# A table prefetch of five items and a rule for empty steps, in a Fourier, mixing and feed-forward kernel on one core

## The chip, the cores and the metric

The kernel runs on one core of a Trainium2 chip. The metric is the device time of one execution in microseconds (us), the median of three runs. The core's engines are called as the profile calls them: PE is TensorE (matrix products; PEld its weight loads), DVE is VectorE, ACT is ScalarE, POOL is GpSimd, SP is SyncE, which here does nothing but issue transfers. Each engine works through its own queue of instructions in order; the engines wait for each other by semaphores.

## The reference: what is computed

```python
X = np.fft.rfft(x, axis=1)                  # x: 8 batches x 3072 x 256
Yr = Xr @ w_r - Xi @ w_i + b_r
Yi = Xr @ w_i + Xi @ w_r + b_i
Yr = np.sign(Yr) * np.maximum(np.abs(Yr) - lam, 0.0)      # lam = 0.01; Yi alike
y = np.fft.irfft(Yr + 1j * Yi, n=3072, axis=1)
h = y.reshape(-1, 256) @ w_in               # 256 x 2048, float64 weights
g = h * np.tanh(softplus(h))
out = g @ w_out                             # 2048 x 256, float64 weights
```

Each of eight batches is transformed along its 3072 rows, mixed by two complex 256 x 256 products, cut softly at 0.01, transformed back, and sent through a feed-forward layer of width 2048.

## The kernel before, in words

**Precision.** Products run on pairs: a 32-bit value is split into `hi` (rounded to the engine's float32r format) and `lo` (the rest). `split` (L185) makes a pair: the copy that rounds (L187 on VectorE, L189 on ScalarE), then the subtraction that gives `lo` (L190, VectorE).

**The transform of a batch** is a `chain` of four segments, each a list of items:

- first (k = 0): 7 items `item_a`, products of x with a small table, result to DRAM scratch s1;
- second (k = 1): 12 items `item_b` (one block of frequencies each, with a table `tt` of 256 KB from DRAM, two tables for block 11, which comes first), each followed one place later by an `item_m` (mix, cut off, store y to scratch s3). The 24 items stand as b11, b0, m11, b1, m0, b2, m1 and so on;
- third (k = 2): 13 items `item_c` (first half of the way back; four or more loads each from s3, result to scratch s2);
- fourth (k = 3): `item_f` 0 and 1 (second half of the way back, with a table `vt`; result `yh`, `yl` in SBUF). There are 12 such items in a batch, two for each chunk of 512 rows.

An item has `load` (its transfers, on SP's queue), `cload` (its table, on POOL's queue), `prep` (the split) and `mm` (one or two groups of matmuls with what follows them). The tables `tt` and `vt` share a pool of four buffers (`p_t`), the loads after the first batch one of four (`p_ld`).

**`run_chain` (L696)** sets the order. It is a generator: each `yield` is one step. For every segment it issues the first loads and tables, then yields empty steps, then calls `prep` of the first one or two items, yields empty steps again (the line of the change), and then takes one `mm` group per step; ahead of each item `ahead` calls `load`, `cload` and `prep` of later items: `ahead_n` loads, `cla` tables, two preps ahead (one in the first segment).

**The first batch** (b = 0) runs alone, from L838 on, with `gap` 0 (no empty steps), `ahead_n` 6 and `cla` 3. The tables of the second segment's first three items are called early, when 11 steps are done. Between the steps, VectorE turns the float64 weights into pairs (`aux_steps`). In this batch half of each item's y stores go over POOL's queue, the queue that also carries the tables.

**The main loop (L867)** then runs over tiles t, 96 per batch (six chunks of 16 tiles). Tile t has `ffn1(t)`: six matmuls of L748 on one 128-column block of `w_in`, and the activation `s`; on even tiles the split of `s` for two tiles (L762, L763); one step of transform work; and `ffn2(t - 4)`: four pairs of matmuls of L778 and L779. The step of transform work comes from one of two generators:

- `gen`, the chain of the next batch, started at the batch's first tile with `gap` 2; its fourth segment is held back until tile 82 of the batch;
- `extra`, a chain of one segment with one item: in tiles 2 and 8 of each of the first five chunks, items `item_f` 2 to 11 of the running batch, also with `gap` 2. In a tile in which `extra` has a real step, `gen` has none; in its empty steps `gen` goes on.

```python
c = tt // KFF
if tt % KFF in (2, 8) and c < 5:
    extra = run_chain([[item_f(b, 2 * c + 2 + (tt % KFF) // 8)]], gap=2)
```

The schedule is written out by hand: the order of calls is the order of each engine's queue. All SP transfers of both generators and of the output stand in one queue.

Of the kernel before, what the change touches and what calls it, by code (L numbers as in the profile page):

```python
# [128 lines left out]
def fft_mix_ffn_kernel(ctx: ExitStack, tc: tile.TileContext, x, w_r, w_i, b_r, b_i, w_in, w_out,  # L129
# [71 lines left out]
    def setup_dft():  # L201
        nc.gpsimd.dma_start(out=fa, in_=c_fa)

    def setup_u():
        nc.gpsimd.dma_start(out=uu, in_=c_u)
# [3 lines left out]
    def load_mix():  # L209
        for k in range(2):  # L210
            t = p_y.tile([128, 2, 512], F32, tag=("yh", "yl")[k], name="wraw").rearrange("p a f -> p (a f)")[:, 0:512]
            nc.sync.dma_start(out=t[:, 0:256], in_=w_r[k * 128:(k + 1) * 128, :])
            nc.sync.dma_start(out=t[:, 256:512], in_=w_i[k * 128:(k + 1) * 128, :])
            mixraw.append(t.rearrange("p (s c) -> p s c", s=2))
# [5 lines left out]
    def setup_mix():  # L220
        for k in range(2):
            src = mixraw[k]
            hi, lo = wmix[:, k, 0, 1:3, :], wmix[:, k, 1, 1:3, :]
            split(src, hi, lo, "s")
            for s in range(2):
                nc.scalar.activation(out=wmix[:, k, s, 0, :], in_=f32(wmix[:, k, s, 2, :]), func=ACTF.Copy, scale=-1.0)
# [55 lines left out]
    def weight_jobs():  # L282
        def w1(k, n):
            sl = slice(n * 512, (n + 1) * 512)
            return (w_in.bitcast(I32)[k * 128:(k + 1) * 128, n * 1024:(n + 1) * 1024],
                    *(win[:, k, s, sl].rearrange("p (a c) -> p a c", a=2) for s in range(2)), False)

        def w2(n):
            return (w_out.bitcast(I32)[n * 256:(n + 1) * 256, :].rearrange("(k p) c -> p k c", p=128),
                    *(wout[:, 2 * n:2 * n + 2, s, :] for s in range(2)), True)  # L290

        order = [w1(0, 0), w1(1, 0), w1(0, 1), w1(1, 1), w2(0), w2(1), w1(0, 2), w1(1, 2), w2(2), w2(3),
                 w1(0, 3), w1(1, 3), w2(4), w2(5), w2(6), w2(7)]
        return [FromDouble(n, *a) for n, a in enumerate(order)]
# [15 lines left out]
    def tick():  # L310
        while pend:
            pend.pop(0)()
# [368 lines left out]
    def chain(b):  # L681
        segs = [[item_a(b, p) for p in range(7)]]
        bm = []
        order = [11] + list(range(11))
        bs = [item_b(b, k) for k in order]
        for k in range(12):
            bm.append(bs[k])
            if k:
                bm.append(item_m(b, order[k - 1], bs[k - 1]))
        bm.append(item_m(b, order[11], bs[11]))  # L690
        segs.append(bm)
        segs.append([item_c(b, p) for p in (*range(8), 12, *range(8, 12))])
        segs.append([item_f(b, 0), item_f(b, 1)])
        return segs

    def run_chain(segs, ahead_n=3, ahead_a=2, cla=2, gap=0, hold=None, on_seg=None):  # L696


        for k, seg in enumerate(segs):
            while hold is not None and k == len(segs) - 1 and hold():  # L700
                yield None
            n = len(seg)
            at = [0, 0, 0]
            la, pla = (ahead_a, 1) if k == 0 and n == 7 else (ahead_n, 2)

            def ahead(i):
                for s, (d, f) in enumerate(((la, "load"), (cla, "cload"), (pla, "prep"))):
                    while at[s] < min(n, i + d):
                        getattr(seg[at[s]], f)()
                        at[s] += 1  # L710

            while at[1] < min(n, cla):
                seg[at[1]].cload()
                at[1] += 1
            while at[0] < min(n, la):
                seg[at[0]].load()
                at[0] += 1
            if on_seg is not None:
                on_seg(k)
            last = k == len(segs) - 1  # L720
            for _ in range(gap + (4 if k == 2 else 1 if last else 0) if gap else 0):
                yield None
            while at[2] < min(n, pla):
                seg[at[2]].prep()
                at[2] += 1
            for _ in range((2 if last or k == 1 else 1) if gap else 0):
                yield None
            for i in range(n):
                ahead(i + 1)
                for f in seg[i].mm:  # L730
                    tick()
                    f()
                    yield k
            tick()
# [59 lines left out]
    with tc.manual_schedule():  # L794
        setup_dft()
        aux = weight_jobs()
        top = [2]
        n_raw = [0]

        def aux_load(m):  # L800
            while n_raw[0] < min(m, len(aux)):
                aux[n_raw[0]].load()
                n_raw[0] += 1

        def aux_run():
            for n, job in enumerate(aux):
                aux_load(n + 1)
                for k, _ in enumerate(job.work(aux[n - 1] if n else None)):
                    if k == 5:
                        aux_load(min(n + (4 if n + 3 <= N_EARLY else 3), top[0]))  # L810
                    yield
            yield from aux[-1].finish()

        aux_gen = aux_run()
        n_aux = [0]

        def aux_steps(m):
            for _ in range(m):
                if started[0] or n_aux[0] < 9 * N_EARLY - 2:
                    next(aux_gen, None)  # L820
                    n_aux[0] += 1

        def on_seg(k):
            if k == 1:
                top[0] = N_EARLY
                aux_load(4)
                setup_mix()
                aux_steps(6)
            elif k == 2:
                aux_steps(12)  # L830
            elif k == 3:
                aux_steps(10)

        PACE = (1.6, 0.9, 1.4, 2)
        first = chain(0)
        cnt = 0
        owed = 0.0
        for k in run_chain(first, ahead_n=6, ahead_a=3, cla=3, on_seg=on_seg):  # L838
            cnt += 1
            if cnt in (2, 6):  # L840
                aux_load(1 + (cnt > 2))
            if cnt == 8:
                load_mix()
                load_bias()
            if cnt == 11:
                for it in first[1][:3]:
                    it.cload()
            if cnt == 20:
                setup_u()
            if cnt == 57:  # L850
                for it in first[3]:
                    it.cload()
            if cnt > 4:
                owed += PACE[k]
            while owed >= 1:
                aux_steps(1)
                owed -= 1
        aux_steps(9 * len(aux))
        started[0] = True
        top[0] = len(aux)  # L860

        LAG = 4
        NT = NCH * KFF
        NS = 6 * KFF
        gen = None
        extra = None
        for t in range(NT + LAG):  # L867
            tt = t % NS
            b = t // NS
            if t == 0:  # L870
                aux_load(N_EARLY + 2)
            if t < 18:
                aux_steps(3)
            if t == 18:
                aux_steps(18)
                mix_gauss()
            if t < NT:
                if tt == 0:
                    gen = run_chain(chain(b + 1), gap=2, hold=lambda: hold[0]) if b + 1 < NB else None
                hold = [tt < 5 * KFF + 2]  # L880
                ffn1(t)
# [3 lines that stand above are left out]
            if t % 2 == 0 and t // 2 - 1 in s_t:  # L885
                split_g(t // 2 - 1, t < 18)
            did = None
            if extra is not None:
                did = next(extra, -1)
                if did == -1:  # L890
                    extra = did = None
            if did is None and gen is not None and t < NT:
                did = next(gen, -1)
                if did == -1:
                    gen = None
            if t < NT and tt == NS - 1 and gen is not None:
                hold = [False]
                for _ in gen:
                    pass
                gen = None  # L900
            if t >= LAG:
                ffn2(t - LAG)
# [26 lines left out]
```

## Time and profile before

| | us |
|---|---|
| median of three runs | 2815.71 (2812.26 to 2817.09) |
| profiled execution | 2812.9 |
| its span | 2811.1 |
| TensorE busy | 2739.7 (97%) |
| VectorE busy | 1952.8 (69%) |
| ScalarE busy | 951.2 (34%) |
| chain that ended last: share of TensorE | 87% |

The busy time of an engine is the time in which at least one of its instructions ran. TensorE's matmuls overlap in their pipeline, so one matmul's duration is longer than the distance to the next. In a list of waits, "A <- B" says that A stood idle until B had ended. In a timeline, an instruction's idle time before it stands in brackets with what ended it; "x2" says that two alike were merged.

### The profile page before, as it was taken

Reading aid. Unit: us, or ns where it says so; the run is one execution under the profiler, and the core shown is the slowest. Engines: PE = TensorE matmul, PEld = TensorE weight load, DVE = VectorE, ACT = ScalarE, POOL = GpSimd, SP = SyncE. Lnnn points to the kernel's source line nnn. Section 1 sums busy time; section 2 is a strip of 40 time slices with the busy share of each in tenths; the row PEclk is TensorE's granted clock in tenths of the full one; section 3 lists DMA queues with packets and bytes.
Section 4 is the critical chain, followed back from the end, with each engine's and each line's share of the span. In section 5 each row is a group of like instructions: output and inputs, shape, how many; then the busy total and the mean of one; then the engine's idle time right before and its main releaser. Section 6 shows DMA issues by size and latency. Waiting matters only on the chain.

```text
span 2811.1 us, 39281 instructions
## 1 busy us (share of the span) xinstructions
PE 2739.7 (97%) x14782; PEld 2333.5 (83%) x14782; DVE 1952.8 (69%) x3294; ACT 951.2 (34%) x1947; POOL 148.0 (5%) x274
## 2 busy tenths in 40 slices
PE   6779999999999999999999999999999999999999
PEld 5558888888888888888888888888888888888887
DVE  5788866778667776678766777567766778655553
ACT  4333333333333333333333333323333333333232
POOL 1400000000000000000000000000000000000000
PEclk9789999999999999999999999999999999999999
DMA  7643324333233323342233332433324333231000
GB/s 223 204 143 86 94 70 120 102 90 94 72 112 109 99 80 86 101 121 84 76 106 102 104 84 68 120 106 87 90 75 120 98 91 91 78 95 42 27 27 16
DMA packets 170388, 266.38 MB, mean 95 GB/s; under 512 B 22518, under 2 KB 67590, under 8 KB 170198
## 3 DMA queue, kind: packets, MB, share of 16 engines
q1 hardware_dynamic: 122806, 173.75, 20.6%
q0 software_dynamic: 33536, 64.95, 8.6%
q10 hardware_dynamic: 13856, 25.17, 3.1%
q8 instruction: 117, 1.92, 0.3%
q14 instruction: 73, 0.60, 0.1%
HBM read 163.10 MB, written 100.68 MB: 94 GB/s over the span
## 4 chain that ended last, share of the span: by engine, by line
PE 87%; DVE 5%; DMA 3%; SPq 2%; issue 1%; ACT 1%; POOL 0%; ACTq 0%; DVEq 0%; POOLq 0%
PE hp L748 35%; PE acc L778 23%; PE acc L779 12%; PE psp L518 4%; PE psa L345 2%; PE psc L626 2%; SPq L604 2%; PE psk L499 2%; PE psf L666 2%; PE psb L434 2%; DMA ld<-in_x_dram 1%; DMA ld<-s 1%; PE psf L667 1%; DVE lo L190 1%; PE psb L436 1%
## 5 line engine op out<-in xcount | busy, mean ns | idle before, releaser
L778 PE MATMUL acc<-wout,gh 128*128 128x512 f32 x3072 | 1115.7, 397 | 0.0
L748 PE MATMUL hp<-yh,win 128*128 128x512 f32 x3072 | 1082.1, 393 | 4.9 <-ACT yh L675 4.6
L753 ACT ACTIVATE s<-hp 128x512 f32<-128x512 f32 x768 | 458.5, 597 | 1368.7 <-PE hp L748 1283.3
L779 PE MATMUL acc<-wout,gl 128*128 128x256 f32 x3072 | 859.2, 280 | 0.0
L748 PEld LDWEIGHTS hp<-yh,win 128*128 128x128 f32 x3072 | 578.6, 188 | 137.4 <-ACT yh L675 4.8
L778 PEld LDWEIGHTS acc<-wout,gh 128*128 128x128 f32 x3072 | 576.6, 188 | 123.4 <-issue 6.0
L748 PE MATMUL hp<-yl,win 128*128 128x512 f32 x1536 | 604.1, 393 | 0.0
L779 PEld LDWEIGHTS acc<-wout,gl 128*128 128x128 f32 x3072 | 577.5, 188 | 16.3
L763 DVE TENSOR_TENSOR gl<-s,gh 128x1024 fp32r<-128x1024 f32 x384 | 470.5, 1225 | 65.3 <-PE acc L779 26.1
L762 DVE CAST gh<-s 128x1024 fp32r<-128x1024 f32 x376 | 258.7, 688 | 207.1 <-ACT s L753 207.1
L748 PEld LDWEIGHTS hp<-yl,win 128*128 128x128 f32 x1536 | 289.2, 188 | 35.0 <-DVE yl L676 0.4
L190 DVE TENSOR_TENSOR lo<-ld,hi 120x512 fp32r<-120x512 f32 (+3 forms) x390 | 269.7, 692 | 31.8 <-ACT hi L189 16.3
L187 DVE CAST hi<-ld 120x512 fp32r<-120x512 f32 (+2 forms) x367 | 154.7, 422 | 56.5 <-DMA ld<-s 55.5
L670 DVE TENSOR_TENSOR eo<-psf,cor 128x256 f32<-128x256 f32 x192 | 76.9, 422 | 117.5 <-ACT cor L669 116.8
L783 DVE TENSOR_TENSOR ot<-acc,oc 128x256 f32<-128x256 f32 x192 | 72.8, 420 | 98.2 <-ACT oc L782 98.2
L650 POOL DMA_DIRECT2D vt<-in_c_v_dram x96 | 52.5, 547 | 1609.4 <-PE psf L667 1261.1
L518 PE MATMUL psp<-wmix,xh 128*128 128x256 f32 x672 | 133.2, 281 | 0.0
L676 DVE TENSOR_TENSOR yl<-yt,yh 128x512 fp32r<-128x512 f32 x96 | 66.5, 693 | 67.1 <-ACT yh L675 67.1
L518 PEld LDWEIGHTS psp<-wmix,xh 128*128 128x128 f32 x672 | 109.1, 188 | 3.6
L675 ACT ACTIVATE yh<-yt 128x512 fp32r<-128x512 f32 x96 | 60.7, 632 | 145.4 <-DVE yt L673 145.4
L626 PE MATMUL psc<-hi,uu 120*120 120x512 f32 (+1 forms) x224 | 89.0, 412 | 17.2 <-ACT hi L189 14.8
L666 PE MATMUL psf<-vt,hi 128*128 128x256 f32 x384 | 95.4, 325 | 7.5 <-ACT hi L189 7.5
(114 smaller groups left out, 2630.5 us busy)
## 6 DMA issues: line engine op xcount, KB each, us to landing
ld<-s SPq DMA_DIRECT2D x185, 256.0 KB
tt<-in_c_t_dram POOLq DMA_DIRECT2D x104, 256.0 KB, 3.2
vt<-in_c_v_dram POOLq DMA_DIRECT2D x96, 256.0 KB, 3.0
out_dram<-ot SPq DMA_DIRECT2D x48, 512.0 KB
ld<-in_x_dram SPq DMA_DIRECT2D x90, 240.0 KB
s<-ev ACTq DMA_DIRECT2D x89, 240.0 KB
s<-y SPq DMA_DIRECT2D x330, 64.0 KB
ld<-s SPq DMA_DIRECT2D x350, 60.0 KB
```

Source lines behind the costliest of these rows:

```text
L187: nc.vector.tensor_copy(out=hi, in_=src)
L190: nc.vector.tensor_tensor(out=lo, in0=src, in1=f32(hi), op=ALU.subtract)
L518: nc.tensor.matmul(out=it.ps[:, ri * 256:(ri + 1) * 256], lhsT=m[:, c, 130 - ri * 128:258 - ri * 128], rhs=wmix[:, c, s, 2 * ri, :], start ...
L626: nc.tensor.matmul(out=ps[:K, sl], lhsT=uu[:K, var, s, :K], rhs=m[:K, sl], start=n == 0, stop=n == 2)
L666: nc.tensor.matmul(out=ps[:, p], lhsT=it.hi[:, q:q + 128], rhs=it.v[:, p], start=True, stop=False)
L670: nc.vector.tensor_tensor(out=eo[:, c], in0=ps[:, :, 0], in1=cor, op=ALU.add)
L748: nc.tensor.matmul(out=hp, lhsT=win[:, k, s, f * 128:(f + 1) * 128], rhs=m[:, k, :], start=n == 0, stop=n == 5)
L753: nc.scalar.activation(out=s_t[t // 2][:, t % 2, :], in_=hp, func=ACTF.Mish)
L762: nc.vector.tensor_copy(out=gh, in_=s)
L763: nc.vector.tensor_tensor(out=gl, in0=s, in1=f32(gh), op=ALU.subtract)
L778: nc.tensor.matmul(out=p, lhsT=gh[:, t % 2, o:o + 128], rhs=wout[:, f], start=f == 0, stop=False)
L779: nc.tensor.matmul(out=p[:, 0], lhsT=gl[:, t % 2, o:o + 128], rhs=wout[:, f, 0], start=False, stop=last)
```

## The change: what it does

Three lines.

```diff
@@ run_chain
-            for _ in range((2 if last or k == 1 else 1) if gap else 0):
+            for _ in range((2 if k else 1) if gap else 0):
                 yield None
@@ first batch
-        for k in run_chain(first, ahead_n=6, ahead_a=3, cla=3, on_seg=on_seg):
+        for k in run_chain(first, ahead_n=6, ahead_a=3, cla=5, on_seg=on_seg):
...
             if cnt == 11:
-                for it in first[1][:3]:
+                for it in first[1][:5]:
                     it.cload()
```

The first sets the number of empty steps between a segment's first `prep` and its first `mm`, for chains with a gap. `last` is true when k is the index of the chain's last segment. The table gives the number by segment:

| chain | segment | before | after |
|---|---|---|---|
| `gen` | k = 0 | 1 | 1 |
| `gen` | k = 1 | 2 | 2 |
| `gen` | k = 2 | 1 | 2 |
| `gen` | k = 3 (last) | 2 | 2 |
| `extra` | k = 0 (last) | 2 | 1 |

The other two set, for the first batch alone, how many items ahead `cload` is called, and how many items' tables are called early. Among the first five items of the second segment are three blocks (11, 0 and 1), which have four tables together.

## Rows read from the trace of the kernel before

**Rows 1.** Windows: busy us (instructions) of each engine, granted clock, DMA share, GB/s.
```profile
158.00:240.00 82.00, 70.92 (x323) 55.21 (x324) 72.69 (x127) 32.40 (x56) 5.47 (x9) 0.96 0.40 114
240.00:2811.00 2571.00, 2562.47 (x14025) 2202.50 (x14023) 1771.39 (x2967) 860.18 (x1785) 96.49 (x179) 1.00 0.30 87
```
**Rows 2.** Waits of TensorE from 260 us on: us in total, times, longest.
```profile
PE psc L626 <- DVE hi L187: 2.3, 6, 0.5
PE psc L626 <- DVE lo L190: 1.2, 7, 0.2
```
**Rows 3.** Timeline of SP's queue, 395 to 440 us: start, us, instruction.
```profile
408.71 9.66 SPq L604 DMA_DIRECT2D ld<-s  x12
418.41 0.56 SPq L644 DMA_DIRECT2D ld<-s  x1
```
**Rows 4.** Timeline of VectorE, 409 to 432 us.
```profile
422.15 0.43 DVE L187 CAST hi<-ld 128x512 fp32r<-128x512 f32 x1 [5.16 <-DMA ld<-s]
422.62 0.69 DVE L190 TENSOR_TENSOR lo<-ld,hi 128x512 fp32r<-128x512 f32 x1
```
**Rows 5.** Timeline of TensorE, 419.2 to 425 us.
```profile
420.64 0.40 PE L778 MATMUL acc<-wout,gh 128*128 128x512 f32 x1
...
423.41 0.29 PE L666 MATMUL psf<-vt,hi 128*128 128x256 f32 x1
```
**Rows 6.** Line L644 (load of item_f): who waited for it, us, times.
```profile
  DVE hi L187: 35.4, 7
```
**Rows 7.** Timeline of VectorE, 2436 to 2444 us.
```profile
2442.61 0.69 DVE L190 TENSOR_TENSOR lo<-ld,hi 128x512 fp32r<-128x512 f32 x1
```
**Rows 8.** Timeline of TensorE, 2438.5 to 2444 us.
```profile
2440.76 0.40 PE L778 MATMUL acc<-wout,gh 128*128 128x512 f32 x1
```
**Rows 9.** Timeline of VectorE, 1372 to 1376 us.
```profile
1374.08 0.69 DVE L190 TENSOR_TENSOR lo<-ld,hi 128x512 fp32r<-128x512 f32 x1
```
**Rows 10.** Timeline of TensorE, 1370 to 1375.5 us.
```profile
1374.69 0.29 PE L518 MATMUL psp<-wmix,xh 128*128 128x256 f32 x1
```
**Rows 11.** Timeline of VectorE, 205 to 209 us.
```profile
206.74 0.69 DVE L190 TENSOR_TENSOR lo<-ld,hi 128x512 fp32r<-128x512 f32 x1
```
**Rows 12.** Timeline of TensorE, 201 to 220 us.
```profile
206.38 0.49 PE L345 MATMUL psa<-hi,fa 120*120 120x512 f32 x1 [3.17 <-DVE raw L269]
```
**Rows 13.** Timeline of VectorE, 495 to 506 us.
```profile
501.07 0.69 DVE L676 TENSOR_TENSOR yl<-yt,yh 128x512 fp32r<-128x512 f32 x1 [0.70 <-ACT yh L675]
```
**Rows 14.** Timeline of TensorE, 504.5 to 507 us.
```profile
505.67 0.39 PE L748 MATMUL hp<-yl,win 128*128 128x512 f32 x1
```
**Rows 15.** Timeline of POOL, 60 to 95 us.
```profile
67.51 1.00 POOL L564 DMA_DIRECT2D s<-y  x2 [3.07 <-DVE y L475]
...
69.06 0.56 POOL L400 DMA_DIRECT2D tt<-in_c_t_dram  x1
```
**Rows 16.** Timeline of TensorE, 64 to 80 us.
```profile
65.26 0.44 PE L535 MATMUL psm<-wmix,xh 128*128 128x512 f32 x1
...
68.10 0.33 PE L422 MATMUL psb<-tt,hi 128*128 128x128 f32 x2
...
73.91 0.41 PE L422 MATMUL psb<-tt,hi 128*128 128x128 f32 x2 [1.53 <-DMA tt<-in_c_t_dram]
...
75.27 0.68 PE L535 MATMUL psm<-wmix,xh 128*128 128x512 f32 x1
...
79.67 0.33 PE L422 MATMUL psb<-tt,hi 128*128 128x128 f32 x2
```
**Rows 17.** Timeline of VectorE, 40 to 106 us.
```profile
79.87 0.69 DVE L473 TENSOR_TENSOR y<-psm,bias 128x512 f32<-128x512 f32 x1 [2.00 <-PE psm L535]
...
93.13 0.69 DVE L473 TENSOR_TENSOR y<-psm,bias 128x512 f32<-128x512 f32 x1 [0.26 <-PE psm L535]
```
**Rows 18.** Windows, as in the first group, of two stretches before 240 us.
```profile
5.00:20.00 15.00, 9.64 (x27) 6.58 (x27) 3.46 (x5) 4.12 (x7) 2.47 (x5) 1.00 1.08 299
205.00:210.00 5.00, 3.62 (x18) 3.05 (x19) 3.88 (x8) 3.04 (x5) 0.00 (x0) 1.00 0.62 187
```

## The prediction

> **What bounds the kernel now.** I read the windows first, by stage. From 240 us to the end TensorE is busy in 2562.47 of 2571 us at a granted clock of 1.00 [rows 1]; the list of TensorE's waits names only two groups in this whole stretch, 2.3 us in 6 waits and 1.2 us in 7, all on VectorE's split of the third stage's inputs [rows 2]. So in this part every microsecond for which TensorE is made to wait is a microsecond of the end, and at most 3.5 us is there to be won. Before 240 us it is otherwise: from 158 to 240 us VectorE is busy in 72.69 of 82 us and TensorE in 70.92 [rows 1].
>
> The edit of the yield count has two users, and they go opposite ways. The condition was "two empty steps if this is the last segment or the second". It becomes "two if this is not the first". A chain of a whole batch gains one empty step, in its third segment (k = 2). But the fourth-stage items 2 to 11 of each batch run as chains of a single segment: there k = 0 and it is the last one as well, so they had two empty steps between `prep` and matmuls and will have one. That is 80 items, whose matmuls go one tile earlier into TensorE's queue while their load and their split stay where they are.
>
> **The change part by part.**
>
> *Item 10 of the fourth stage, batches 0 to 6.* Its load is issued in tile 66 of the batch, its split in tile 69, its matmuls in tile 71, now 70. One tile ahead of it, in tile 65, the next batch's third stage puts its first three loads into the same SP queue: three items of four transfers, 12 in all, which leave SP one after the other in 9.66 us, and item 10's load can only leave behind them, at 418.41 [rows 3]. VectorE has been idle for 5.16 us when the data land; the cast starts at 422.15, and `lo` ends at 422.62 + 0.69 = 423.31 [rows 4]. TensorE reaches item 10 today at 423.41, just after that. The matmuls of tile 70 (counted along the queue, six of L748 to a tile) give way to the next instruction at 420.64 [rows 5], and that is where item 10 will stand. Its first matmul needs `hi` (422.58), its second `lo`, so TensorE stands still for about 423.31 - 420.64 = 2.67 us. This is no accident of one batch: seven such splits waited for their load, 35.4 us together [rows 6], and in the last of them `lo` ends at 2442.61 + 0.69 = 2443.30 [rows 7] against 2440.76 on TensorE [rows 8], 2.54 us. Read in the same way the seven give 2.67, 2.56, 2.55, 2.17, 3.10, 2.39 and 2.55, together 18.0 us; in the fifth batch TensorE waits 0.2 us already today, so 17.8 are new. Nothing gives them back, since TensorE waits for nothing else downstream. Lower bound: if only `hi` mattered, 0.73 us less each, 12.9 us.
>
> *Other single items.* Item 8 is next in line: 1374.08 + 0.69 = 1374.77 on VectorE [rows 9] against 1374.69 on TensorE [rows 10], 0.1 us in each of seven batches, 0.7 us. For every other item from batch 1 on, read in the same way, `lo` is done before TensorE would ask for it. Items 2 and 3 of batch 0 fall into the stretch before 240 us, where VectorE is behind: item 3's `lo` ends at 206.74 + 0.69 = 207.43 [rows 11], and TensorE, free from 206.38 - 3.17 = 203.21, waits until 206.38 today for another VectorE result [rows 12], so 1.05 us are new there. If TensorE decided this stretch, I would allow the whole 207.43 - 203.21 = 4.2 us for the two items; if VectorE does, whose work stays the same, nothing. I take 0.5, near the second, because VectorE is the busier [rows 1].
>
> *Third stage, one tile more.* `prep` of items 0 and 1 stays, the matmuls come 2.8 us later: the waits of [rows 2] go: minus 3.5 us. What comes late next is the end of the chain: the fourth stage's items 0 and 1 of the next batch move from tiles 92 and 93 to 93 and 94, and the first layer needs their result in tile 96. Today `yl` ends at 501.07 + 0.69 = 501.76 [rows 13], and its first reader comes at 505.67 [rows 14]. One tile later (2.8 us), and with 1.1 us more because the split of `s` now stands ahead of it on VectorE, `yl` ends near 505.6 (an estimate, from the order of VectorE's instructions in these tiles). That cover is thin; I count nothing, with 0.7 us (0.1 in seven batches) as upper end. No DMA is delayed by it: the loads of the third stage hang on buffers that `prep` frees, and `prep` does not move.
>
> *Tables of the first batch, five ahead.* On POOL a table's load stands behind the y stores of the item before it: POOL waits for VectorE, issues two stores at 67.51, a weight load, and only at 69.06 the table [rows 15] for which TensorE then waits 1.53 us [rows 16]. Two items earlier in the order, the load passes one pair of stores, some 4 us. The pool has four buffers; the one that each load takes has been free since four blocks before, so the earlier call is not held up, except for the first two, which wait for block 11 today too. TensorE gains this wait, a shorter one, and a slow stretch behind it: item 4's matmuls take 79.67 - 75.27 = 4.40 us, where the same twelve took 68.10 - 65.26 = 2.84 [rows 16]. But VectorE ends this stage, and it stood idle for TensorE only twice, 2.00 and 0.26 us [rows 17]: the gain is at most 2.3 us; I take 2.0. Against it, one more table (256 KB) now lies among the first stage's x loads, where the DMA engines are full at 299 GB/s [rows 18]: up to 0.26 MB / 299 GB/s = 0.9 us later, less what its later place now gains by its absence; 0.5. Sum -1.5, ends -2.3 and +0.9.
>
> Sum: 17.8 + 0.7 + 0.5 - 3.5 - 1.5 = **+14.0 us**. The profiled execution took 2812.9 us (span 2811.1 and 1.8 around it), 2.8 below the median of the three runs; the mean of these four is 2814.5, on which I put the sum: **2828.5 us**.
>
> **Rivals.**
>
> *The clock falls behind each new wait.* For: after the 1.53 us wait at 73.91 the twelve matmuls cost 1.56 us more [rows 16]. Against: after a wait of 3.17 us [rows 12], longer than any of the new ones, the granted clock stayed at 1.00 from 205 to 210 us [rows 18]. If it fell behind all seven: 7 x 1.56 = 10.9 us more, 2839.4. [...]
>
> *Item 10's data come in time after all; then the kernel is not slower.* The one mechanism is SP's queue: if the load left 2.8 us earlier against TensorE, the matmuls would find their data. For that at least four of the twelve transfers (0.8 us each) would have to move behind it, or the y stores ahead of them come earlier. The change moves neither, and the order is fixed; so this is unlikely. Then only 0.5 - 3.5 - 1.5 = -4.5 us is left (item 8 going the same way): 2810.0.
>
> *The tables do nothing.* If the earlier call waits for a buffer at every block, or VectorE takes up the gain, the sum is +15.5 to +16.4: about 2830.5.
>
> **Chances.** Forecast 0.66, tables without effect 0.16, clock 0.09, data in time 0.09. A change of this kernel under 0.2% (5.6 us) can hardly be told from none. Faster by more needs the last of these at its best: 0.04. Within 0.2%: the rest of that case, and the lower tail of the first two: 0.10. Slower: 0.86. Range: below, `hi` alone (12.9 us, with 3.5 and 2.3 us off and a little more) gives +5, 2819; above, all upper ends give 17.8 + 0.7 + 4.2 + 0.7 + 0.9 - 3.5 = +20.8, 2835.3, and the clock case 2839.4: I take 2840.
>
> **What would show it.** Right: a new group in the list of TensorE's waits, psf (L666, L667) on VectorE's `hi` and `lo` of L187 and L190, 7 long waits and some 18 us, each some 85 us ahead of the next batch's first tile (505.67 - 420.64); psc on L187 gone from 240 us on; no psb wait on a table; the hp matmuls of a batch's first tile without a new wait on `yl`. Wrong: psf waits under 1 us, or a table still late, or a granted clock under 1.00 behind the new waits. If the time falls under 2815 with the long psf waits present, the claim that TensorE makes up nothing is wrong.

## The result, and the profile after

The changed kernel takes 2833.64 us (median of 6 runs, 2832.35 to 2835.41) against 2815.82 us before (6 runs, 2812.26 to 2817.96): a ratio of 1.0063, interval 1.0052 to 1.0074. It is slower, by 17.8 us by the medians. The profiled execution took 2832.35 us with a span of 2830.5, which is 19.4 us longer than the span before.

The page of the changed kernel, the line of busy times and the line of the chain of work that ended last:

```profile
PE 2751.1 (97%) x14782; PEld 2339.8 (83%) x14782; DVE 1943.9 (69%) x3294; ACT 953.3 (34%) x1947; POOL 147.0 (5%) x274
...
PE 86%; DVE 5%; DMA 4%; SPq 3%; issue 1%; ACT 1%; ACTq 0%; DVEq 0%; POOLq 0%
```

The page alone would lead nowhere: TensorE is busy 97% of the span before and after. The windows of the changed kernel by stage, with the columns of [rows 1]:

```profile
158.00:240.00 82.00, 72.28 (x324) 56.89 (x323) 71.05 (x124) 30.84 (x54) 5.54 (x9) 0.93 0.39 114
240.00:2830.00 2590.00, 2569.77 (x14018) 2206.27 (x14016) 1761.41 (x2965) 861.92 (x1785) 95.56 (x179) 1.00 0.30 87
```

Before, TensorE stood idle for 2571 - 2562.47 = 8.5 us from 240 us on [rows 1]; now for 20.2 us. The list of its waits in that stretch, in the place of [rows 2] (us in total, times, longest):

```profile
PE psf L666 <- DVE hi L187: 11.8, 7, 2.1
PE psf L667 <- DVE lo L190: 2.4, 7, 0.3
PE psa L345 <- DVE eva L354: 1.4, 3, 0.7
```

The two psc groups of [rows 2] are gone. Seven waits of psf, one per batch, have come, and a third, small group. One of the seven, followed through three engines. SP's queue of the changed kernel (compare [rows 3]):

```profile
407.34 9.67 SPq L604 DMA_DIRECT2D ld<-s  x12
417.05 0.56 SPq L644 DMA_DIRECT2D ld<-s  x1
```

VectorE of the changed kernel (compare [rows 4]):

```profile
420.65 0.43 DVE L187 CAST hi<-ld 128x512 fp32r<-128x512 f32 x1 [5.01 <-DMA ld<-s]
421.11 0.69 DVE L190 TENSOR_TENSOR lo<-ld,hi 128x512 fp32r<-128x512 f32 x1
```

TensorE of the changed kernel (compare [rows 5]):

```profile
419.05 0.39 PE L748 MATMUL hp<-yh,win 128*128 128x512 f32 x1
421.13 0.39 PE L666 MATMUL psf<-vt,hi 128*128 128x256 f32 x1 [1.69 <-DVE hi L187]
421.86 0.33 PE L667 MATMUL psf<-vt,lo 128*128 128x128 f32 x1 [0.34 <-DVE lo L190]
422.02 0.40 PE L666 MATMUL psf<-vt,hi 128*128 128x256 f32 x1
...
423.18 0.73 PE L778 MATMUL acc<-wout,gh 128*128 128x512 f32 x1
...
425.72 0.39 PE L748 MATMUL hp<-yh,win 128*128 128x512 f32 x1
```

Load and split stand where they stood, behind the same twelve transfers, and only the matmuls asked a tile earlier. The first L666 follows the end of the cast (420.65 + 0.43 = 421.08), the first L667 the end of `lo` (421.80). The four pairs of L778 and L779 behind them then take 425.72 - 423.18 = 2.54 us. In another tile a pair takes 0.36 us (436.11 to 436.47 in a view further down), so four take 1.4. The windows show what goes with it; the first is the stretch behind this wait, the second the one behind the same wait of the third batch:

```profile
422.00:425.50 3.50, 3.50 (x14) 3.21 (x15) 3.06 (x6) 1.04 (x3) 0.53 (x1) 0.52 0.45 119
...
1102.00:1105.50 3.50, 3.16 (x19) 2.71 (x20) 3.36 (x7) 0.77 (x2) 0.53 (x1) 1.00 0.39 91
```

The granted clock is 0.52 in the one (0.50, in what follows the lower level, in nearly all of it) and 1.00 in the other. Four of the seven waits, those of the first, second, fourth and sixth batch, have such a stretch of some 3.5 us behind them; three have none.

To divide the 19.4 us I took the start of each tile's first L748 in both traces and subtracted. Listed waits are no substitute: they count from modelled ends of matmuls that overlap (a matmul of 0.40 us has the next one 0.24 us behind its start, 435.17 to 435.41 in a view further down). All seven batches together:

| stretch | after - before, us |
|---|---|
| up to tile 0 of the first batch | -3.3 |
| tiles 0 to 62 of the first batch (items 2 and 3) | +1.9 |
| tiles 66 to 73 (item 10): 4.13, 4.61, 2.48, 3.97, 2.31, 3.96, 2.46 | +23.9 |
| tiles 73 to 96 (third stage's first item, ends of the chain) | -6.8 |
| tiles 0 to 30 of the following batch | +3.2 |
| tiles 30 to 66 (item 8) | +0.5 |
| last batch, from its tile 10 on | 0.0 |

The three undisturbed batches lose 2.48, 2.31 and 2.46 us, 2.42 in the mean; seven times that is 16.9. The four with the low clock lose 16.67 together, 7.0 more than 4 x 2.42, that is 1.75 us each.

### The profile page after: what moved, and what is told of

It is laid out like the page before. It is cut to its first block, busy times and chain, and to the rows that moved or that the text cites. A ratio compares the mean times of both kernels' runs of the same rounds, so it can differ in the third digit from the quotient of the medians.

```text
span 2830.5 us, 39238 instructions
## 1 busy us (share of the span) xinstructions
PE 2751.1 (97%) x14782; PEld 2339.8 (83%) x14782; DVE 1943.9 (69%) x3294; ACT 953.3 (34%) x1947; POOL 147.0 (5%) x274
## 4 chain that ended last, share of the span: by engine, by line
PE 86%; DVE 5%; DMA 4%; SPq 3%; issue 1%; ACT 1%; ACTq 0%; DVEq 0%; POOLq 0%
PE hp L748 34%; PE acc L778 23%; PE acc L779 12%; PE psp L518 4%; SPq L604 2%; PE psc L626 2%; PE psk L499 2%; PE psf L666 2%; PE psa L345 2%; PE psb L434 2%; DMA ld<-s 1%; DMA s<-eva 1%; PE psf L667 1%; DMA ld<-in_x_dram 1%; DVE lo L190 1%
## 5 line engine op out<-in xcount | busy, mean ns | idle before, releaser
L778 PE MATMUL acc<-wout,gh 128*128 128x512 f32 x3072 | 1120.4, 398 | 0.0
L748 PE MATMUL hp<-yh,win 128*128 128x512 f32 x3072 | 1084.5, 394 | 5.3 <-ACT yh L675 4.6
L779 PE MATMUL acc<-wout,gl 128*128 128x256 f32 x3072 | 861.7, 280 | 0.0
L748 PEld LDWEIGHTS hp<-yh,win 128*128 128x128 f32 x3072 | 580.0, 189 | 138.8 <-ACT yh L675 4.8
L778 PEld LDWEIGHTS acc<-wout,gh 128*128 128x128 f32 x3072 | 579.0, 188 | 123.8 <-issue 6.0
L748 PE MATMUL hp<-yl,win 128*128 128x512 f32 x1536 | 605.3, 394 | 0.0
L779 PEld LDWEIGHTS acc<-wout,gl 128*128 128x128 f32 x3072 | 580.0, 189 | 16.4
L748 PEld LDWEIGHTS hp<-yl,win 128*128 128x128 f32 x1536 | 289.7, 189 | 35.7 <-DVE yl L676 0.4
L190 DVE TENSOR_TENSOR lo<-ld,hi 120x512 fp32r<-120x512 f32 (+3 forms) x390 | 269.7, 692 | 30.5 <-ACT hi L189 16.9
L187 DVE CAST hi<-ld 120x512 fp32r<-120x512 f32 (+2 forms) x367 | 154.1, 420 | 56.2 <-DMA ld<-s 56.2
L666 PE MATMUL psf<-vt,hi 128*128 128x256 f32 x384 | 99.2, 331 | 24.3 <-DVE hi L187 11.8
L473 DVE TENSOR_TENSOR y<-psp,y 128x512 f32<-128x512 f32 x84 | 58.0, 691 | 79.9 <-PE psp L518 79.2
L354 DVE TENSOR_TENSOR eva<-psa,s2nd 120x512 f32<-120x512 f32 (+1 forms) x98 | 64.2, 684 | 59.7 <-DMA s<-eva 42.6
```

Source lines behind the costliest of these rows:

```text
L187: nc.vector.tensor_copy(out=hi, in_=src)
L190: nc.vector.tensor_tensor(out=lo, in0=src, in1=f32(hi), op=ALU.subtract)
L666: nc.tensor.matmul(out=ps[:, p], lhsT=it.hi[:, q:q + 128], rhs=it.v[:, p], start=True, stop=False)
L748: nc.tensor.matmul(out=hp, lhsT=win[:, k, s, f * 128:(f + 1) * 128], rhs=m[:, k, :], start=n == 0, stop=n == 5)
L778: nc.tensor.matmul(out=p, lhsT=gh[:, t % 2, o:o + 128], rhs=wout[:, f], start=f == 0, stop=False)
L779: nc.tensor.matmul(out=p[:, 0], lhsT=gl[:, t % 2, o:o + 128], rhs=wout[:, f, 0], start=False, stop=last)
```

## The experiments

All edits are against the kernel before, unless said otherwise. Ratios are to the kernel before on the same chip.

**The tables alone.**

```diff
-        for k in run_chain(first, ahead_n=6, ahead_a=3, cla=3, on_seg=on_seg):
+        for k in run_chain(first, ahead_n=6, ahead_a=3, cla=5, on_seg=on_seg):
...
-                for it in first[1][:3]:
+                for it in first[1][:5]:
```

> The kernel before with the two table edits alone (five ahead, five called early). My theory: TensorE's waits for tables in the second stage are gone, the feed-forward part starts 3.3 us earlier, and nothing after it changes: about -3.3 us, 2812.5. Rival (the gain is given back before the feed-forward part's end, where VectorE sets the pace from 158 to 240 us): the start is 3.3 us earlier but the time within 0.5 us of before.

Measured: 2809.05 us (2807.69 to 2812.05, 11 runs) against 2815.27, ratio 0.9981 (0.9972 to 0.9990), a gain of about 5 to 6 us. No wait on a table is left between 50 and 108 us. From 240 us on the two psc groups are still there, as they must be:

```profile
PE psc L626 <- DVE hi L187: 1.7, 5, 0.4
PE psc L626 <- DVE lo L190: 1.2, 7, 0.2
```

**The single items alone**, one empty step for them, the third segment and the tables as before.

```diff
-            for _ in range((2 if last or k == 1 else 1) if gap else 0):
+            for _ in range((2 if k in (1, 3) else 1) if gap else 0):
```

> The kernel before with one empty step instead of two for the single items alone; the third segment keeps its one, the tables stay three ahead. My theory: TensorE waits for item 10 in seven batches (14 us together), runs at half clock behind some of these waits (about 1.6 us each), and stands 1.8 us longer at items 2 and 3 of the first batch; the third segment's own waits (3.5 us) vanish because TensorE comes later: +21 us, 2837. Rival (the edits add up independently): the third segment's waits stay, +24.5 us.

Measured: 2835.88 us (2833.22 to 2838.06, 5 runs), ratio 1.0075 (1.0062 to 1.0089), +20.6. The list of TensorE's waits from 240 us on:

```profile
PE psf L666 <- DVE hi L187: 11.6, 7, 1.9
PE psf L667 <- DVE lo L190: 2.4, 7, 0.3
PE psa L345 <- DVE eva L354: 1.1, 2, 0.9
```

So this half of the condition holds the whole loss, with the same seven waits. The psc groups are gone here too, though the third segment kept its one empty step: TensorE, late from item 10, comes to the third stage after the split has ended. In tiles 66 to 73 this trace loses 22.2 us and in tiles 73 to 96 it wins 6.5. With the single items late, the third segment's extra step brings nothing of its own.

**The third segment alone**, the single items back at two empty steps.

```diff
-            for _ in range((2 if last or k == 1 else 1) if gap else 0):
+            for _ in range((2 if last or k else 1) if gap else 0):
```

> The kernel before with the second empty step for the third segment alone; the single items keep their two. My theory: the waits of psc on VectorE from 240 us on (3.5 us) go and no wait takes their place: -3.5 us, 2812.3. Rival: the end of the chain, one tile later, makes the first layer wait for yl, 0.3 to 1 us in each of seven batches: -1.5 to +3.5 us.

Measured: 2809.38 us (2806.64 to 2812.06, 10 runs) against 2815.27, ratio 0.9978 (0.9968 to 0.9988), -5.9; 3.5 us was too little. The list of TensorE's waits from 240 us on is empty. The size is in the distances. The kernel before, TensorE at the third stage's first item:

```profile
434.25 0.40 PE L748 MATMUL hp<-yh,win 128*128 128x512 f32 x1
434.48 0.40 PE L626 MATMUL psc<-hi,uu 120*120 120x512 f32 x1
...
435.18 0.40 PE L778 MATMUL acc<-wout,gh 128*128 128x512 f32 x1
```

This is an item with its data there: 435.18 - 434.25 = 0.93 us from the matmul ahead to the one behind. The same view one tile earlier, where the first item waits:

```profile
429.64 0.39 PE L748 MATMUL hp<-yh,win 128*128 128x512 f32 x1
430.51 0.46 PE L626 MATMUL psc<-hi,uu 120*120 120x512 f32 x1 [0.48 <-DVE hi L187]
431.14 0.49 PE L626 MATMUL psc<-lo,uu 120*120 120x512 f32 x1 [0.18 <-DVE lo L190]
...
431.71 0.39 PE L778 MATMUL acc<-wout,gh 128*128 128x512 f32 x1
```

Here it is 2.07 us, so the wait costs 1.14 where the brackets say 0.48 + 0.18 = 0.66. And the changed kernel at its first item:

```profile
435.17 0.40 PE L748 MATMUL hp<-yh,win 128*128 128x512 f32 x1
435.41 0.40 PE L626 MATMUL psc<-hi,uu 120*120 120x512 f32 x1
...
436.11 0.40 PE L778 MATMUL acc<-wout,gh 128*128 128x512 f32 x1
...
436.47 0.40 PE L778 MATMUL acc<-wout,gh 128*128 128x512 f32 x1
```

0.94 us. From tile 73 to tile 96, all seven batches together, the gain is 6.5 us in this experiment and 6.8 in the changed kernel.

**Tables and third segment together**: the last edit and the first one.

> Both table edits and the third segment's second empty step, the single items with two empty steps as before. My theory: the two gains add up, -6.8 us, 2809, better than both kernels; no wait of TensorE is listed from 240 us on. Rival (something else than the single items makes the changed kernel slower): at or above 2815.

Measured: 2804.95 us (2801.98 to 2805.82, 5 runs) against 2815.27, ratio 0.9961 (0.9948 to 0.9974). The two gains add up (5.3 and 6.2 by their ratios, 11.0 together), and this version beats both kernels. Its window from 240 us on:

```profile
240.00:2803.00 2563.00, 2558.16 (x14017) 2201.79 (x14016) 1766.99 (x2964) 857.11 (x1785) 96.31 (x179) 1.00 0.30 87
```

TensorE is idle for 4.8 us of 2563, and its list of waits there is empty.

**The changed kernel with one load moved.** Is it SP's queue that makes item 10's data late? Edit against the changed kernel: item 10's load is issued at the top of tile 64, ahead of the twelve loads of the next batch's third stage.

```diff
+                if tt == 4 * KFF:
+                    early = item_f(b, 10)
+                    early.load()
+                    early.load = lambda: None
...
-                    extra = run_chain([[item_f(b, 2 * c + 2 + (tt % KFF) // 8)]], gap=2)
+                    nb = 2 * c + 2 + (tt % KFF) // 8
+                    extra = run_chain([[early if nb == 10 else item_f(b, nb)]], gap=2)
```

> The changed kernel with one thing moved: item 10's load is called at the top of tile 64, ahead of the twelve loads of the third stage on SP's queue. My theory (SP's queue holds item 10's load back, and that alone makes the kernel slower): TensorE's waits for item 10 and the half clock behind them are gone, 20.7 us less than the changed kernel: 2813. Rival (the earlier place of the matmuls costs by itself, whatever the load does): 2833 within 3.

Measured: 2809.25 us (2808.31 to 2811.39, 10 runs) against 2815.29, ratio 0.9981 (0.9971 to 0.9990). By moving one 0.5 us issue in each batch the loss has become a gain, 3.8 us larger than expected. SP's queue of this kernel:

```profile
401.24 0.52 SPq L644 DMA_DIRECT2D ld<-s  x1
...
409.77 9.66 SPq L604 DMA_DIRECT2D ld<-s  x12
```

And its TensorE, with no wait between the first layer and item 10:

```profile
421.49 0.40 PE L748 MATMUL hp<-yh,win 128*128 128x512 f32 x1
421.72 0.29 PE L666 MATMUL psf<-vt,hi 128*128 128x256 f32 x1
```

The list of its waits from 240 us on has one line left, the small group that the changed kernel has too:

```profile
PE psa L345 <- DVE eva L354: 2.0, 3, 1.1
```

Tiles 66 to 73 differ from the kernel before by -0.4 us over all seven batches. The cause of the 23.9 us is thereby shown.

**Item 10 alone at one empty step, and at none.** `run_chain` gets a parameter `rest`, the number of empty steps in the last segment:

```diff
-            for _ in range((2 if last or k == 1 else 1) if gap else 0):
+            for _ in range((rest if last else 2 if k == 1 else 1) if gap else 0):
...
-                    extra = run_chain([[item_f(b, 2 * c + 2 + (tt % KFF) // 8)]], gap=2)
+                    nb = 2 * c + 2 + (tt % KFF) // 8
+                    extra = run_chain([[item_f(b, nb)]], gap=2, rest=1 if nb == 10 else 2)
```

The second of the two has `rest=0 if nb == 10`.

> The kernel before with one empty step for item 10 alone; all other single items keep two. My theory: seven waits of about 2 us, 14 us together, plus 0 to 11 us of half clock behind them (four of seven fell in the changed kernel: 6.6), less 3.5 us of third-segment waits that vanish: +17 us, 2833. Rival (each of the ten single items of a batch bears its part): +2 us.

Measured, one step: 2830.4 us (2826.01 to 2841.18, 5 runs) against 2815.29, ratio 1.0058 (1.0036 to 1.0079), +15.1. Item 10 by itself makes the loss. Its waits from 240 us on are those of the singles:

```profile
PE psf L666 <- DVE hi L187: 11.7, 7, 1.9
PE psf L667 <- DVE lo L190: 2.4, 7, 0.3
```

Its runs lie further apart than those of any other kernel here. The profiled one (2839.53) is near the top, and in it the clock fell behind all seven waits: tiles 66 to 73 lose 5.71, 5.75, 5.63, 3.74, 3.82, 3.95 and 4.19 us, 32.8 together, for the same 14 us of listed waits. In the first three batches the lower level lasts for about 7 us, in the other four for about 3.5.

> The kernel before with no empty step for item 10 alone: its matmuls two tiles earlier than before, the wait doubled. My theory: each wait grows by a tile of 2.8 us, 14.2 + 7 x 2.8 = 34 us, less 3.5, plus the half clock behind each of the waits if longer waits make it fall more often (up to 7 x 1.6 = 11): +30 to +42 us. If the fall does not depend on the length of the wait, about four of seven again: +37 us. Rival (TensorE catches up on a wait within the batch): no more than +20.

Measured, no step: 2863.67 us (2856.65 to 2864.66, 4 runs), ratio 1.0167 (1.0152 to 1.0183), +48.4, more than the upper end. The list of waits from 240 us on:

```profile
PE psf L666 <- DVE hi L187: 31.4, 7, 4.7
PE psf L667 <- DVE lo L190: 0.3, 1, 0.3
```

The stretch behind the first of them, TensorE and then the window:

```profile
422.85 0.39 PE L748 MATMUL hp<-yh,win 128*128 128x512 f32 x1
427.69 0.58 PE L666 MATMUL psf<-vt,hi 128*128 128x256 f32 x1 [4.45 <-DVE hi L187]
...
429.97 0.73 PE L778 MATMUL acc<-wout,gh 128*128 128x512 f32 x1
```

```profile
425.20:432.20 7.00, 4.37 (x15) 3.79 (x16) 2.73 (x6) 1.09 (x3) 0.53 (x1) 0.51 0.50 162
```

The granted clock is still 1.00 from 423.50 to 425.20 us, inside the wait, then 0.51 over these 7 us, and low for as long at each of the seven waits. Tiles 66 to 73 lose 53.3 us, 21.9 more than the listed 31.4, that is 3.1 per batch. The expectation had allowed 1.6 us per wait for the clock, read from a shorter slow stretch, and nothing for the part of a stall that the list leaves out.

**The two table edits one by one.** First the early call alone:

```diff
-                for it in first[1][:3]:
+                for it in first[1][:5]:
```

> The kernel before with the early call of five items' tables alone (three ahead later on). My theory: one table moves from 38 us to about 8 us; the second stage's first matmul starts 0.5 us earlier, since the table no longer lies beside the last stores of the first stage, and TensorE's two waits for tables (2.2 us) stay. Rival (the first stage's x loads are held up by the table): 0.5 us later.

Measured: 2814.57 us in the single run, against 2815.29. Block 11 starts at 46.10 us against 47.35 before, but kernels without this edit show 46.73 to 47.23 as well. Over all traces it starts at 46.1 to 46.8 us in the five with the early call (mean 46.4) and at 46.7 to 47.4 in the six without (mean 47.0). A wait on a table stays (1.6 us), and a single run shows no gain in the time. Then five ahead alone:

```diff
-        for k in run_chain(first, ahead_n=6, ahead_a=3, cla=3, on_seg=on_seg):
+        for k in run_chain(first, ahead_n=6, ahead_a=3, cla=5, on_seg=on_seg):
```

> The kernel before with tables five ahead alone, three called early as before. My theory (TensorE's waits for tables in the second stage, 3.5 to 4.2 us in the kernels with tables three ahead that were profiled since, with the half clock behind them, are the larger share of the tables' 6 us): -4 to -5 us, and the second stage's first matmul where it was before, at 47 us within 0.4. Rival (the early call alone brings the gain, by the end of the first stage): within 1.5 us of before, and a wait of psb for a table still in the list.

Measured: 2809.58 us (2807.13 to 2812.54, 11 runs) against 2816.74, ratio 0.9978 (0.9969 to 0.9987). The whole gain of the tables is in this one number. The waits on a table between 50 and 108 us are 2.2 us in the kernel before, none here, and 4.2 in the kernel with the single items alone, whose tables are those of before:

```profile
PE psb L422 <- DMA tt<-in_c_t_dram: 4.2, 2, 2.2
```

The window 70 to 85 us of the kernel before, of the single items alone, and of five ahead, in this order:

```profile
70.00:85.00 15.00, 13.47 (x71) 11.26 (x69) 12.70 (x24) 3.65 (x7) 5.37 (x10) 0.89 0.67 198
```

```profile
70.00:85.00 15.00, 12.79 (x60) 10.90 (x59) 10.72 (x21) 2.86 (x5) 4.82 (x10) 0.77 0.63 193
```

```profile
70.00:85.00 15.00, 14.86 (x88) 12.90 (x88) 14.72 (x29) 4.82 (x8) 6.41 (x12) 1.00 0.78 223
```

With five ahead VectorE is busy in 14.72 of 15 us, with 12.70 and 10.72 in the others, and the clock stays up (1.00 against 0.89 and 0.77). It stays up in one trace without the edit too, that of item 10 at one step (1.00, VectorE busy 13.89). The first L748 of tile 0 starts at 154.1 to 157.9 us in the five traces with five ahead (mean 156.4) and at 158.2 to 164.4 in the six without (mean 161.9; the early call alone is one of them): 5.5 us. The kernel before, at 158.19, has the earliest start of the six. These starts go along with the clock: up to tile 0 TensorE is granted the lower level for 60.0 to 67.5 us in the five traces (mean 64.0) and for 65.8 to 77.2 in the six (mean 71.4), least in the earliest of all and most in the latest. How much of the 5.5 us is the clock's share and how much the waits' is not shown.

## Why the prediction was right, and which of its terms were not

The time lies in the range, 5 us above the forecast, and the sign has the cause that was named. That the total came so near is in part luck: the terms differ more than their sum.

| term | predicted | by the traces |
|---|---|---|
| item 10, waits | +17.8 | +16.9 |
| item 10, clock behind the waits | 0 (rival: 10.9) | +7.0 |
| other single items (item 8) | +0.7 | +0.5 |
| items 2 and 3 of the first batch | +0.5 | +1.9 |
| third stage | -3.5 | -6.8 |
| tables | -1.5 | -3.3 in this trace, about -5.5 over all |
| `yl` ahead of the first layer, tiles 0 and 1 of the following batch | 0, at most 0.7 | +0.5 |
| waits on eva and the like, tiles 2 to 30 | not named | +2.7 |

*Item 10* came as worked out, place, number and size; the 16.9 us is an estimate, seven times the mean of the three batches with full clock. The load moved ahead of the twelve transfers removes it, and item 10 alone reproduces it. The slack read from VectorE's timeline against TensorE's queue (2.55, 2.90 and 2.55 for the three batches with full clock) was good to 0.1 us in two cases and 0.6 in the third; the batch missed is the fifth, for a reason that stays open. Only the view named for it shows less than announced: 14.2 us in the list of waits in place of some 18, since the list counts from modelled ends.

*The clock* was wrong as a choice between all or nothing. The prediction priced two cases, that it fell behind all seven waits and that it does not fall, took the second, and named a low clock behind the waits as what would prove it wrong; it fell behind four here, three with the single items alone, and all seven in both kernels that moved item 10 alone. The price of 1.56 us per fall that was read from [rows 16], where the granted clock was 0.61 from 75.27 to 79.67 us, is near the 1.75 measured here, but no upper end: with item 10 alone at one step a fall cost 1.3 to 3.3 us, 15.9 in all (32.8 - 16.9) against the 10.9 of that rival.

*The third stage* failed in the step that set what can be won equal to the sum of the listed waits, 3.5 us. That sum counts idle time only, and modelled ends hide part of a stall. From tile to tile the same stretch won 6.8 us. Nor is this gain the extra step's own in the changed kernel: item 10 alone at one step wins the same 6.8 us there with the third segment as before. The two terms were added as if independent, but a TensorE that has lost time at item 10 does not meet these waits. What was to come late next, `yl`, came as near as estimated. VectorE and then TensorE of the changed kernel at the next batch's first tile:

```profile
506.51 0.69 DVE L676 TENSOR_TENSOR yl<-yt,yh 128x512 fp32r<-128x512 f32 x1 [0.70 <-ACT yh L675]
```

```profile
507.31 0.44 PE L748 MATMUL hp<-yl,win 128*128 128x512 f32 x1
```

`yl` ends at 507.20, 0.11 us ahead of its first reader. No wait is listed, but tiles 0 and 1 lose 0.5 us over seven batches, 0.4 to 0.6 in the other three kernels with the extra step and nothing in those without it.

*The tables* failed in the cap. The 2.0 us came from VectorE's idle time in one execution, the one that came to tile 0 earliest of the six without the edit; against their mean the gain is 5.5. The 0.5 us against it does not show either: with the early call block 11 starts some 0.7 us earlier, by the means above.

*Items 2 and 3* were priced near the lower end because VectorE is the busier engine there. TensorE of the changed kernel stands at item 3:

```profile
205.61 0.55 PE L666 MATMUL psf<-vt,hi 128*128 128x256 f32 x1 [5.37 <-ACT s2nd L350]
```

That is a longer stop than the 3.17 us of [rows 12], and the wait on `lo` is not what is listed. The traces with one empty step for all single items lose 1.4 to 1.9 us from tile 0 to tile 62 against the kernel before, and those without lie between 1.3 less and 0.2 more: some 2.2 us apart by their means, inside the 0 to 4.2 given.

*Not named at all* were the tiles after a batch's start, where a single item now comes ahead of an item of the first stage; the psa group on eva is listed only in kernels with one step for all single items. The two kernels that move item 10 alone differ by less than 0.3 us in these tiles, so item 10's lateness is not the cause; that the swap is, is argued, not tried.

The errors cancel in part: 7.0, 2.7, 1.4 and 0.5 us too little cost on one side, and on the other 0.9 and 0.2 too much cost and 3.3 and 1.8 too little gain. What is left, 5.4 us, is the distance of this trace's 19.4 from the 14.0 of the sum. With the two gains alone sized rightly the forecast would have been further off.

## What to carry to other kernels

Before taking slack out of a step, look at what stands ahead of its load in the queue that issues it: here one condition with two users took a tile away from seven loads that leave behind 9.7 us of other transfers, and the slack that looked spare was what hid them. Price a stall of TensorE from the start of the matmul ahead to the start of the one behind, not from listed idle time, and add the chance of a slower stretch behind it (in the changed kernel four waits of seven, 1.75 us each). Where a stage varies between executions, one profile gives no cap: look at the same stage in several.

## What the runs showed of the hardware

The granted clock fell to its lower level, 0.50, behind waits of 1.5 to 2.2 us in four of seven cases in the changed kernel. The wait's length does not tell which: the listed waits on `hi` were 1.69, 2.15, 1.52 and 1.50 us where it fell and 1.61, 1.77 and 1.57 where it did not. At the waits of about 4.5 us of item 10 without an empty step it fell in all seven, but so it did in the profiled run of item 10 at one step, behind 1.3 to 1.9 us. What decides in the shorter ones stays open. How long it stayed down differs as well: where it was about 3.5 us a batch lost 3.7 to 4.6 us in tiles 66 to 73, where it was about 7 us 5.6 to 5.8, with alike listed waits. It matters for reading times: with the same listed waits of 14 us, the kernels with item 10 a tile early lost 22.2, 23.9 and 32.8 us in tiles 66 to 73.
